# One weight transfer for two, dummy matmuls up to its landing, and one repeated matmul pair fewer

## The chip, the cores and the metric

The kernel runs on one core of a Trainium2 chip. The metric is the device time of one execution in microseconds (us). Timed runs of one kernel are compared with runs of the kernel before in the same rounds, on the same chip. "Span" is the length of one profiled execution; times within it count from its start.

## The reference, cut to what matters

```python
# x: [1, 384, 384, 384], dw: [1, 1, 384], pw: [384, 384], all bfloat16; k = 1, so no padding
out = x * dw[0, 0]                                  # depthwise, one tap
return jnp.einsum('bhwc,cd->bhwd', out, pw)         # pointwise: [147456, 384] x [384, 384]
```

The kernel folds dw into pw once, at its start, and then streams x through one matmul with the folded weight.

## The kernel before

Only the head (the first 7 us or so) is touched. SyncE issues pw in two transfers, then x:

```python
nc.scalar.dma_start(dw_row[:], ...).then_inc(s_dw, 16)
nc.sync.dma_start(pw_n[:, 0, :], pw[:P, :]).then_inc(s_pw[0], 16)
nc.sync.dma_start(pw_n[:, 1:3, :], pw[P:, :].rearrange("(k p) d -> p k d", p=P)).then_inc(s_pw[1], 16)
# ... x chunks follow on the same queue
```

TensorE runs dummy matmuls on zeros, and then folds dw into pw. sel_w is a selection matrix scaled by dw; a product of it with pw_n gives the folded weight in PSUM, two tiles of 64 rows at a time (a "pair"), six results in all, numbered i = 2k + r:

```python
idle_work(3)                      # loop, 3 trips of 4 dummy matmuls; needs only zeros
# ... three small matmuls for dw
idle_work(1)
times = {(1, 1): 3, (2, 0): 3}    # pairs that are repeated to keep TensorE busy
for k in range(3):
    if k < 2: nc.tensor.wait_ge(s_pw[k], 16)
    nc.tensor.wait_ge(s_sw, k + 1)                 # sel_w of this k
    for r in range(2):
        if k == 2: nc.tensor.wait_ge(*w_done[r])   # its PSUM bank has been copied out
        for v in [0, 1] * times.get((k, r), 1):
            mm = nc.tensor.matmul(PS[(k + 1) % 2][:, 2 * r + v, :D], lhsT=sel_w[...], rhs=pw_n[...], ...)
        mm.then_inc(s_w)
with nc.tensor.Fori(0, NS // 2, 1) as it:          # the body: 288 supertiles of 48 matmuls
    ...
```

Six PSUM-to-SBUF copies make w_r of the results: the second on VectorE, the others on ScalarE, one after another. The body's first matmul waits for the first four copies (they hold its first weights, and two of them free the PSUM banks that it writes) and for the first transpose of x on VectorE. `...` marks cuts.

## Time and profile before

| | us |
|---|---|
| time, three runs at first | 574.9, 575.14, 576.55 |
| time, these three and three more, taken with the changed kernel | median 576.16 |
| span of the profiled execution | 574.1 |
| body's first matmul | 7.21 |
| half-rate stretch of the body, up to full clock at 8.08 | 0.87 |
| start of the last matmul to the end | 5.1 |

TensorE starts its groups of four matmuls 0.30 to 0.32 us apart at first and 0.162 us apart from about 8.1 us on; below these are called half and full rate, or half and full clock.

The page's groups and chain and the head's timeline are shown in the prediction below. A group line reads: source line, engine, operation, tiles, shapes and count, then busy time in us, mean duration in ns, and idle time before the group with what ended most of it. A chain line reads: start, length, what was waited for. In a line of the stretches view each engine's busy time is followed by the number of its instructions that touch the stretch.

### The profile page before, as it was taken

How to read it: one execution, taken by the hardware profiler on the slowest of the kernel's cores; microseconds unless marked ns; L12 is line 12 of the kernel's file. 1: busy time of each engine (PE TensorE's matmuls, PEld its weight loads, DVE VectorE, ACT ScalarE, POOL GpSimd, SP SyncE). 2: the span in 40 equal slices, each digit the busy share in tenths (PEclk: the TensorE clock that was granted, in tenths of full speed). 3: DMA queues.
4: the chain of work that ended last, by engine and by line, in shares of the span. 5: the costliest groups of instructions: out<-in, count | busy, mean ns of one | idle time of the engine just before them, and what ended most of it. 6: DMA issues, size and time to landing. Idle time of an engine off the chain costs nothing.

```text
span 574.1 us, 29692 instructions
## 1 busy us (share of the span) xinstructions
PE 567.5 (99%) x13863; PEld 334.3 (58%) x13863; DVE 508.2 (89%) x583; ACT 419.1 (73%) x296; POOL 0.9 (0%) x8
## 2 busy tenths in 40 slices
PE   8999999999999999999999999999999999999996
PEld 4555555555555555555555555555555555555553
DVE  7889888988988898899889888988988898899884
ACT  6777777777777777777777777777777777777775
POOL 0000000000000000000000000000000000000000
PEclk9999999999999999999999999999999999999999
DMA  8999999999999999999999999999999999995996
GB/s 327 442 404 408 431 415 423 436 429 405 383 411 412 391 400 428 398 390 402 426 385 400 398 430 403 390 393 419 396 395 424 400 388 392 421 397 172 414 386 241
DMA packets 25929, 226.88 MB, mean 395 GB/s; under 512 B 1214, under 2 KB 5695, under 8 KB 22079
## 3 DMA queue, kind: packets, MB, share of 16 engines
q1 hardware_dynamic: 25916, 226.79, 98.1%
q14 instruction: 10, 0.07, 0.0%
q8 instruction: 1, 0.02, 0.0%
q10 hardware_dynamic: 2, 0.00, 0.0%
HBM read 113.54 MB, written 113.25 MB: 395 GB/s over the span
## 4 chain that ended last, share of the span: by engine, by line
PE 98%; DMA 1%; ACT 0%; DVE 0%; SPq 0%; issue 0%
PE ps L167 97%; DMA pw_n<-in_pw_dram 1%; PE ps L218 0%; DMA out_dram<-O 0%; ACT O L309 0%; DVE O L306 0%; SPq L132 0%; SPq L339 0%; SPq L100 0%
## 5 line engine op out<-in xcount | busy, mean ns | idle before, releaser
L167 PE MATMUL ps<-w_r,T 32*128 32x384 bf16 x13824 | 562.2, 321 | 0.0
L260 DVE STREAM_TRANSPOSE T<-X 128x384 uint32<-128x384 uint32 x576 | 505.0, 878 | 56.0 <-DMA X<-in_x_dram 1.4
L309 ACT CAST O<-ps 128x1536 bf16<-128x1536 f32 x288 | 413.6, 1436 | 148.1 <-PE ps L167 148.1
L167 PEld LDWEIGHTS ps<-w_r,T 32*128 32x128 bf16 x13824 | 332.5, 93 | 229.9 <-issue 1.0
L273 ACT CAST w_r<-ps 128x768 bf16<-128x768 f32 x5 | 3.9, 800 | 1.5 <-PE ps L218 1.5
L218 PE MATMUL ps<-pw_n,sel_w 64*128 64x384 bf16 x20 | 3.6, 518 | 0.5 <-DVE sel_w L288 0.3
L306 DVE CAST O<-ps 128x768 bf16<-128x768 f32 x1 | 1.0, 957 | 3.0 <-DMA out_dram<-O 3.0
L184 PE MATMUL ps<-zero 32*128 32x384 bf16 x16 | 1.8, 493 | 1.4 <-POOL zero L234 1.4
L218 PEld LDWEIGHTS ps<-pw_n,sel_w 64*128 64x128 bf16 x20 | 1.2, 131 | 2.6 <-DMA pw_n<-in_pw_dram 1.5
L246 ACT ACT_TABLE_LOAD x1 | 1.3, 1283 | 1.5 <-SPq L100 1.5
L278 DVE TENSOR_REDUCE sel<-eye 128x64 f32<-128x128 bf16 x1 | 0.3, 289 | 1.8 <-POOL eye L236 1.8
L184 PEld LDWEIGHTS ps<-zero 32*128 32x128 bf16 x16 | 0.5, 99 | 2.0 <-issue 2.0
L273 DVE CAST w_r<-ps 128x768 bf16<-128x768 f32 x1 | 1.0, 958 | 0.5 <-PE ps L218 0.5
L288 DVE TENSOR_SCALAR sel_w<-sel,dw_f 128x256 bf16<-128x256 f32 x3 | 0.9, 350 | 0.0
L285 DVE COPY dw_f<-ps 128x3 f32<-128x3 f32 x1 | 0.2, 160 | 0.8 <-PE ps L199 0.8
L236 POOL TENSOR_SCALAR_AFFINE_SELECT eye<-ones 128x128 bf16<-128x128 bf16 x1 | 0.3, 292 | 0.1
L246 ACT COPY warm<-warm 128x1 f32<-128x1 f32 x2 | 0.3, 189 | 0.0
L199 PEld LDWEIGHTS ps<-ones,dw_row 1*128 1x128 bf16 x3 | 0.2, 100 | 0.2 <-issue 0.2
L234 POOL MEMSET zero<- 128x192 uint32 x1 | 0.3, 258 | 0.0
L199 PE MATMUL ps<-ones,dw_row 1*128 1x1 bf16 x3 | 0.2, 160 | 0.0
L235 POOL MEMSET ones<- 128x128 bf16 x1 | 0.2, 204 | 0.0
L328 POOL MEMSET const-bfloat16-1.0<- 128x1 bf16 x1 | 0.1, 102 | 0.0
(4 smaller groups left out, 0.4 us busy)
## 6 DMA issues: line engine op xcount, KB each, us to landing
X<-in_x_dram SPq DMA_DIRECT2D x26, 3840.0 KB, 21.6
out_dram<-O SPq DMA_DIRECT2D x26, 3840.0 KB, 27.6
X<-in_x_dram SPq DMA_DIRECT2D x2, 1536.0 KB, 17.2
out_dram<-O SPq DMA_DIRECT2D x2, 1536.0 KB, 13.8
X<-in_x_dram SPq DMA_DIRECT2D x3, 768.0 KB, 7.6
out_dram<-O SPq DMA_DIRECT2D x3, 768.0 KB, 10.7
X<-in_x_dram SPq DMA_DIRECT2D x1, 2304.0 KB, 19.4
out_dram<-O SPq DMA_DIRECT2D x1, 2304.0 KB, 11.3
```

The lines of the kernel that those rows point to most:

```text
L167: mm = nc.tensor.matmul(PS[s][:, q, :D], lhsT=Ts[s][32 * q : 32 * q + 32, b, par::2], rhs=w_r[32 * q : 32 * q + 32, b, par, :], start=(b, ...
L184: nc.tensor.matmul(PS[0][:, i, :D], lhsT=zero[32 * i : 32 * i + 32, 0:P], rhs=zero[32 * i : 32 * i + 32, :], start=True, stop=True, tile_p ...
L199: mm = nc.tensor.matmul(PS[1][:, 0, D + k : D + k + 1], lhsT=dw_row[:, P * k : P * k + P], rhs=ones[0:1, 0:1], start=True, stop=True,)
L218: mm = nc.tensor.matmul(PS[(k + 1) % 2][:, 2 * r + v, :D], lhsT=sel_w[64 * v : 64 * v + 64, k, r, :, :].rearrange("p q w -> p (q w)"), rhs ...
L234: nc.gpsimd.memset(zero[:].bitcast(U32), 0).then_inc(s_zero)
L236: nc.gpsimd.affine_select(out=eye[:], in_=ones[:], pattern=[[-1, P]], compare_op=mybir.AluOpType.is_equal, fill=0.0, base=0, channel_multi ...
L246: c = nc.scalar.copy(warm[:, s + 1 : s + 2], warm[:, 0:1])
L260: ins = nc.vector.transpose(out=Tw[:, 3 * h : 3 * h + 3], in_=Xw[:, :, j, 96 * h : 96 * h + 96].rearrange("p k (b w) -> p b k w", w=32),)
L273: o = nc.vector.tensor_copy(out, in_) if e == 0 else nc.scalar.copy(out, in_)
L288: nc.vector.tensor_scalar_mul(sel_w[:, k], sel[:].unsqueeze(2).to_broadcast([P, 2, 4, 32]), dw_f[:, k : k + 1]).then_inc(s_sw)
L306: e = nc.vector.tensor_copy(Ov[:, nq:4, j, :], PS[s][:, nq:4, :D])
L309: a = nc.scalar.copy(Ov[:, 0:nq, j, :], PS[s][:, 0:nq, :D])
```

## The change

Its intent, as far as the edit tells: save one transfer issue, and keep TensorE busy without a gap up to the landing of pw, so that its clock comes to full rate earlier; the repeat is then less needed.

```diff
-        nc.sync.dma_start(pw_n[:, 0, :], pw[:P, :]).then_inc(s_pw[0], 16)
-        nc.sync.dma_start(pw_n[:, 1:3, :], pw[P:, :].rearrange("(k p) d -> p k d", p=P)).then_inc(s_pw[1], 16)
+        nc.sync.dma_start(pw_n[:], pw.rearrange("(k p) d -> p k d", p=P)).then_inc(s_pw, 16)
...
-        idle_work(1)
-        times = {(1, 1): 3, (2, 0): 3}
+        idle_work(3)
+        nc.tensor.wait_ge(s_pw, 16)
+        times = {(1, 1): 3, (2, 0): 2}
         for k in range(3):
-            if k < 2:
-                nc.tensor.wait_ge(s_pw[k], 16)
```

More of the change, by code (lines that the diff above doesn't have):

```diff
@@ L89 @@
     s_dw = nc.alloc_semaphore("s_dw")
-    s_pw = [nc.alloc_semaphore(f"s_pw{h}") for h in range(2)]
+    s_pw = nc.alloc_semaphore("s_pw")
     s_df = nc.alloc_semaphore("s_df")
```

## The prediction

> **What bounds the kernel now.** I read three things in this order: the groups of instructions with the chain that ended last (what sets the end), the timeline of the first 8 us (all that the diff touches), then the stretches of the main matmul line (how fast it runs, and from when).
>
> ```profile
> L167 PE MATMUL ps<-w_r,T 32*128 32x384 bf16 x13824 | 562.2, 321 | 0.0
> L260 DVE STREAM_TRANSPOSE T<-X 128x384 uint32<-128x384 uint32 x576 | 505.0, 878 | 56.0 <-DMA X<-in_x_dram 1.4
> ...
> L218 PE MATMUL ps<-pw_n,sel_w 64*128 64x384 bf16 x20 | 3.6, 518 | 0.5 <-DVE sel_w L288 0.3
> ```
>
> The main matmuls (L167) never wait: idle before them is 0.0. VectorE's transposes waited for an x transfer for 1.4 us in all, at the start. So although the DMA engines are busy 0.98 of the span, they keep up, and TensorE sets the pace from its first L167 matmul to its last. The stretch from 100 to 200 us holds 2464 weight loads, four to a group that runs at once on four row tiles: 616 groups in 100 us, 0.1623 us each. 13824 / 4 = 3456 groups x 0.1623 = 561.0 us. What remains of the 574.1 us span is a head of 7.2 us, a tail of 4.7 us (last matmul near 569.4, then copy, store and exit), and about 1 us of slow groups and drain. The change touches neither the 561 nor the tail. Its ceiling is the part of the head that it can shorten, plus matmuls that run at a slow clock.
>
> The chain of waits names the head:
>
> ```profile
> 1.47 3.03 DMA pw_n<-in_pw_dram
> 4.49 0.05 issue
> 4.54 2.74 PE ps L218 x12
> 7.28 558.25 PE ps L167 x11413
> ```
>
> It says second pw transfer, then weight preparation, then body. The timeline shows that this is not the only path into 7.2 us:
>
> ```profile
> 1.01 0.39 SPq L132 DMA_DIRECT2D pw_n<-in_pw_dram  x1
> 1.47 0.42 SPq L133 DMA_DIRECT2D pw_n<-in_pw_dram  x1
> 1.92 3.75 SPq L113 DMA_DIRECT2D X<-in_x_dram  x7
> 2.74 0.51 PE L184 MATMUL ps<-zero 32*128 32x384 bf16 x4
> 3.08 0.88 DVE L288 TENSOR_SCALAR sel_w<-sel,dw_f 128x256 bf16<-128x256 f32 x3
> 3.55 0.16 PEld L218 LDWEIGHTS ps<-pw_n,sel_w 64*128 64x128 bf16 x4 [0.70 <-DMA pw_n<-in_pw_dram]
> 4.54 0.13 PEld L218 LDWEIGHTS ps<-pw_n,sel_w 64*128 64x128 bf16 x4 [0.82 <-DMA pw_n<-in_pw_dram]
> 6.04 0.80 ACT L273 CAST w_r<-ps 128x768 bf16<-128x768 f32 x1 [0.16 <-PE ps L218]
> 6.24 10.29 DVE L260 STREAM_TRANSPOSE T<-X 128x384 uint32<-128x384 uint32 x12 [0.84 <-DMA X<-in_x_dram]
> 7.21 9.03 PE L167 MATMUL ps<-w_r,T 32*128 32x384 bf16 x208
> ```
>
> The first L167 matmul needs three ScalarE copies (the third runs 6.04 to 6.84) and the first transpose, which starts when x lands (6.24) and takes 0.86, so ends at 7.10. The later of the two is the transpose; 7.21 follows it by 0.1 us. The weight path has about 0.27 us to spare. TensorE meanwhile stands idle twice: 3.25 to 3.55, and 4.40 to 4.54, with only loosely packed work before.
>
> **The clock.** The stretches of L167 alone show the rest:
>
> ```profile
> 7.20:8.10 0.90, 0.89 (x12) 0.44 (x16) 1.00 1.01 416
> 8.10:9.00 0.90, 0.90 (x28) 0.55 (x24) 1.00 1.01 423
> ```
>
> The same 0.90 us holds 12 matmuls and then 28. The starts in the trace are 0.30 to 0.32 us apart per group up to 8.12 and 0.162 after it, and the trace's record of full clock begins at 8.08 (the clock column prints 1.00 before it too, so durations are the better witness). So 0.87 us of body ran at half rate in this execution, a loss of 0.87 / 2 = 0.43 us.
>
> **What the Trainium skill says.** "TensorE: Matmul & The Clock Gate", section "Part 1: The HAM clock gate": the array starts at half clock and is released after a busy window of about 3.4 us; the window is free-running, so the moment depends on its phase at kernel start. The trace agrees with the factor of two (0.32 against 0.162 us). It also fits the window: 8.08 less 3.41 is 4.67, just after TensorE became continuously busy at 4.54, while the window 1.25 to 4.66, in which TensorE shows 2.77 us busy of 3.41 with its modelled ends (less in streaming), did not release it. "DMA: Bandwidth & Descriptors", section "Queues, rings and completion order": descriptors of one queue are consumed in ring order, so x comes behind pw. The trace agrees: nearly all 768-byte pw packets finish before the 3072-byte x packets begin. Same page, "Why a DMA increments its semaphore by 16 and not by 1": a transfer is done when its slowest engine is. The trace shows it: of the second pw transfer's landings fifteen are in by 3.88 us and the last at 4.49; of the first x chunk fifteen by 5.53 and the last at 6.22.
>
> **The change part by part.**
> 1. One pw transfer for two. Bytes and packets stay (288 KB, 384 of 768 bytes). SyncE saves one issue: x is issued at about 1.47 instead of 1.92, 0.45 us earlier. But the engines were fed almost without a break from 2.02 us on (the second transfer's packets follow the first's by about 0.1 us, x's first packet comes 6 ns after an engine's pw finished), so I give x only 0.1 to 0.2 us of that: landing near 6.1.
> 2. The first weight matmuls now wait for the whole transfer. Before they were free at 3.43 by sel_w and ran at 3.58; now pw lands in one piece at T. 24 packets per engine x 36 ns = 0.86 us from 2.02, plus the roughly 0.6 us of starting stalls and completion, plus the late engine: T = 3.8 to 4.2 us. From T, the ScalarE path is: two matmul pairs and drain 0.55, copy 0.80, copy 0.80, copy 0.80, so the third copy ends at T + 2.95 to 3.0, i.e. 6.8 to 7.2, against 6.84 before. The weight path gives its slack away, and with a late T it becomes the bound.
> 3. Dummy loop of three in place of one: two more trips at 0.43 us (the spacing of the first loop's weight loads, 1.40, 1.84, 2.27). TensorE is then busy from 2.74 to about 4.1, which covers the wait. They cost nothing unless pw lands before about 4.05, then up to 0.2 us.
> 4. One repeat of the third block's first pair fewer: one pair, 0.32 us at half clock. It comes after what the third copy waits for, so it is off both paths; near zero.
>
> Start of the body: later of transposes (6.1 + 0.86 + 0.1 = 7.06) and weights (6.8 to 7.2, plus 0.1), so 7.1 to 7.2, a gain of 0.05 (range -0.2 to +0.3).
>
> Clock: with TensorE packed from 1.43 on, the first window that counts may begin anywhere within 3.41 us after 1.43 and releases the clock between 4.84 and 8.25, nearly always before the body begins. Before, the packed stretch began at 4.54, so release came between 7.95 and 11.36, by phase. Loss in the body is half of (release - 7.21): 0.37 to 2.07 us, mean 1.2; after, about 0.1. That is an estimate from the window the skill states. The profiled run, with 0.43, would be a lucky one; the spread of the three timed runs before (574.9 to 576.55, 1.65 us wide) is the width this predicts (1.7). The mean of the three is 575.5; less 1.1 for the clock and 0.05 for the start gives 574.4. If the denser head only sometimes passes, it is nearer 574.9. I take 574.5.
>
> **The rivals.**
> *Transfer hidden anyway:* x alone sets 7.21, the clock is released when it was, and nothing moves: 575.1 to 575.5. For it: x's landing is the last event before the body in the trace. Against it: the half-rate groups after 7.21 are real and the change fills the idle time before them.
> *A new wait:* pw in one piece lands late (its slowest engine), the first copy starts 0.5 us later than 4.12 and the third copy passes the transpose. For it: the late engine shows on both transfers. With T = 4.5 the body starts at 7.55: plus 0.35, partly paid back by the clock; 574.8 to 575.8.
> *DMA becomes the bound:* at 0.98 busy a faster TensorE could run into late x or O buffers. Against it: no transpose waits for x after the head, and half to one microsecond in 575 changes no rate. No effect.
> *The dummy work does not suffice:* the loop's branch leaves about 0.11 us in each 0.43, so the window may still fail; then the only effect is the start, 575.0 to 575.5.
>
> **Range and chances.** I give the clock story 0.6, hidden anyway or insufficient dummy work 0.3, a late pw 0.1. Centre 574.5, with phase alone able to move a run by a microsecond and medians of few runs: 573.8 to 575.5. A 2% change would be 11.5 us, more than the whole head; so within 2% at 0.98, and 0.01 on each side for a disturbed run.
>
> **What the profile after would show.** One pw issue, and x issued near 1.47; x landing (first transpose) at 6.0 to 6.2; pw landing near 4.0 with the dummy matmuls running up to it; weight pairs 0.16 us apart instead of 0.32 at least in their later part; the first L167 groups 0.162 apart from the start; L167 busy down from 562.2 to about 561.7; body starting at 7.0 to 7.3 and a tail of 4.7 unchanged. The prediction is wrong if the pairs in the head and the first groups are still 0.32 us apart (dummy work insufficient), if the first copy starts after 4.9 (pw late), or if L167 shows idle time later in the run (transfers now bind).

## The result, and the profile after

Six runs of the changed kernel: 575.22 to 575.92, median 575.36. Six of the kernel before: 574.9 to 576.55, median 576.16. The ratio is 0.9992, with a 95% interval of 0.9979 to 1.0005: the same, within noise. The means are 575.42 and 575.87, 0.45 us apart. The prediction had 574.5, a gain of 1 us over the mean of before's first three runs (575.5). The absolute time falls in its range; the gain that it explained does not appear.

The page of the changed kernel, the groups that answer to those of before:

```profile
L166 PE MATMUL ps<-w_r,T 32*128 32x384 bf16 x13824 | 561.8, 321 | 0.1
L258 DVE STREAM_TRANSPOSE T<-X 128x384 uint32<-128x384 uint32 x576 | 506.2, 882 | 54.0 <-DMA X<-in_x_dram 2.4
...
L216 PE MATMUL ps<-pw_n,sel_w 64*128 64x384 bf16 x18 | 3.0, 510 | 0.1
```

The body's busy time is 561.8 us, as foreseen (561.7), against 562.2. VectorE waits 2.4 us for x instead of 1.4, and the body does not feel it: its idle time is 0.1. The chain of the changed kernel:

```profile
1.01 3.03 DMA pw_n<-in_pw_dram
4.05 0.05 issue
4.09 2.96 PE ps L216 x18
7.05 0.12 issue
7.18 557.91 PE ps L166 x13728
```

The whole of pw lands at 4.04, 0.45 us before the second transfer of the kernel before did; but the weights then take 3.1 us to the body in place of 2.7. The body starts 0.04 us earlier than in the profile before. Its timeline shows why the weights take longer:

```profile
1.01 0.45 SPq L132 DMA_DIRECT2D pw_n<-in_pw_dram  x1
1.52 3.49 SPq L113 DMA_DIRECT2D X<-in_x_dram  x7
2.74 1.28 PE L183 MATMUL ps<-zero 32*128 32x384 bf16 x12
4.09 2.96 PE L216 MATMUL ps<-pw_n,sel_w 64*128 64x384 bf16 x18
4.63 3.80 ACT L271 CAST w_r<-ps 128x768 bf16<-128x768 f32 x5 [1.56 <-PE ps L216]
5.83 1.55 DVE L258 STREAM_TRANSPOSE T<-X 128x384 uint32<-128x384 uint32 x2
7.18 9.12 PE L166 MATMUL ps<-w_r,T 32*128 32x384 bf16 x220
```

ScalarE's first copy starts at 4.63 instead of 4.12, and from there the copies follow each other without a gap (3.80 us for five, none waiting again): three of them end at 7.03. Before, the first copy was under way when the second transfer landed (4.49). VectorE's transpose no longer waits for x (it landed at 5.00) and ends 0.5 us before the body starts. The stretches of the body's line in the changed kernel:

```profile
7.20:8.10 0.90, 0.90 (x24) 0.68 (x28) 1.00 1.06 423
8.10:9.00 0.90, 0.90 (x32) 0.62 (x24) 1.00 0.97 403
```

No thin first stretch: 24 matmuls against 12 before. The trace records full clock from 6.82 us, before the body starts. So in this one execution the body's clock and start went as predicted, and saved 0.43 us of half rate and 0.04 us of start. Two signs did not: the weight pairs stayed 0.32 us apart up to the last one, at 6.63 us, and x landed at 5.00 us where 6.0 to 6.2 was foreseen. The span fell from 574.15 to 573.70, by 0.45. The question is what one execution is worth.

### The profile page after: what moved, and what is told of

Read it like the earlier page. It is cut to its first block, busy times and chain, and to the rows that moved or that the text cites. A ratio compares the mean times of both kernels' runs of the same rounds, so it can differ in the third digit from the quotient of the medians.

```text
span 573.7 us, 29706 instructions
## 1 busy us (share of the span) xinstructions
PE 567.3 (99%) x13869; PEld 414.9 (72%) x13869; DVE 509.3 (89%) x583; ACT 418.8 (73%) x296; POOL 0.9 (0%) x8
## 4 chain that ended last, share of the span: by engine, by line
PE 98%; DMA 1%; ACT 0%; DVE 0%; issue 0%; SPq 0%
PE ps L166 97%; DMA pw_n<-in_pw_dram 1%; PE ps L216 1%; DMA out_dram<-O 0%; ACT O L307 0%; DVE O L304 0%; SPq L337 0%; SPq L100 0%
## 5 line engine op out<-in xcount | busy, mean ns | idle before, releaser
L166 PE MATMUL ps<-w_r,T 32*128 32x384 bf16 x13824 | 561.8, 321 | 0.1
L166 PEld LDWEIGHTS ps<-w_r,T 32*128 32x128 bf16 x13824 | 412.9, 93 | 149.2 <-issue 0.7
```

What stands on the lines that cost most here:

```text
L166: mm = nc.tensor.matmul(PS[s][:, q, :D], lhsT=Ts[s][32 * q : 32 * q + 32, b, par::2], rhs=w_r[32 * q : 32 * q + 32, b, par, :], start=(b, ...
```

## The experiments

In each trace I took four numbers: when pw was complete (the last of its sixteen landings), when the body started, when full clock was granted, and the length of the body from its first matmul's start to its last one's. **The body's length is 561.41 to 561.46 us plus half of its half-rate time in all 17 traces**, with half-rate times from 0 to 2.49 us. So "body start plus half of the half-rate time" is all that the head costs, and I call it the head cost. (Times read from the traces are in part cut, not rounded, at the second decimal, so a view can show 0.01 more.)

The windows of the clock show too: the records of full clock are 566.612, 563.199 and 580.266 us long, which is 166, 165 and 170 times 3.413 us. From a trace's release time (the moment when full clock is granted) I can therefore count back in windows of 3.413 us and work out how busy TensorE was in the window that brought full clock, and in the one before it that didn't. For this I take the first 0.32 us (the spacing of pairs at half clock) after each start of a matmul of 384 columns, counting overlaps once; after a matmul of fewer columns, in proportion less. Their share of the window I call the streaming share. The three one-column matmuls for dw count for nothing in it; had each counted for 0.32 us, as in the expectation of `e5_duty_384`, shares of windows that hold them would be 0.03 higher.

### Control: both kernels again

`c_before` is the kernel before and `c_after` the changed kernel, both without an edit.

> The kernel before, unchanged, as a control and for a second trace of its head. Both theories: ratio 1.000 within 0.002. Clock theory (the moment of full clock is random against the kernel's start, and before loses time to it): the runs spread over 1 to 2 us, and in this new trace full clock comes at another time than 8.08 us, somewhere in 4.7 to 11.4. Landing theory (the spread comes from late DMA engines in the head): the clock comes near 8.1 again, and the start of the body moves from 7.21 to anywhere in 6.4 to 7.3 with the landings of x and of the second pw transfer.

> The changed kernel, unchanged, for more runs and a second trace. Clock theory: full clock at another time than 6.82 us, within 4.8 to 8.3, so nearly no half-rate groups in the body; runs within 0.8 us of each other, 0.5 to 1 us below before on average (ratio 0.9983 to 0.9992). Landing theory: body starts 3.1 us after pw lands, ratio 0.999 to 1.001.

Measured: the unchanged copy of before has a ratio of 1.0013 to before (0.9993 to 1.0034), the changed kernel 1.0009 (0.9993 to 1.0025). A kernel compared with itself is off by 0.13%, 0.75 us; so the times cannot settle half a microsecond, and the traces must. Two expectations on the times failed here: the runs of the copy of before spread over 3.8 us in place of 1 to 2, and those of the changed kernel over 3.1 us in place of 0.8, with a ratio above the 0.9983 to 0.9992 foreseen. Full clock came at 9.35 us in the copy of before, in place of 8.08, and at 7.93 in the changed kernel, in place of 6.82: the moment is a matter of chance. The stretches of the body in the copy of before:

```profile
7.20:8.10 0.90, 0.90 (x16) 0.40 (x20) 1.00 1.02 423
8.10:9.00 0.90, 0.90 (x16) 0.41 (x12) 1.00 1.03 430
9.00:9.90 0.90, 0.90 (x24) 0.53 (x20) 1.00 1.11 464
```

Two thin stretches and part of a third: 2.24 us at half rate, 1.12 us lost. But the window from 2.52 to 5.94 us in that trace had a streaming share of 0.74 and did not bring full clock, and in the changed kernel the window from 1.11 to 4.52, with 0.73, did not either.

In this copy x landed at 5.42 us and its first transpose ended at 6.31, yet the body started at 7.11. So x is not what sets the start. In both traces of before the start is 2.72 us after the second landing of pw (4.49 and 4.39), and 0.46 us after the start of TensorE's last weight pair. The chain of the copy says the same:

```profile
4.44 2.74 PE ps L218 x16
7.18 558.92 PE ps L167 x12607
```

### The transfer alone, and the filling alone

`e1_one_transfer` is the changed kernel with the dummy loop and the repeat of before:

```diff
-        idle_work(3)
+        idle_work(1)
         nc.tensor.wait_ge(s_pw, 16)
-        times = {(1, 1): 3, (2, 0): 2}
+        times = {(1, 1): 3, (2, 0): 3}
```

> The merged transfer alone: dummy loop of one, third repeat kept. TensorE then stands idle from 3.25 to about 4.0 us. If the dummy matmuls carry the gain (clock theory): 0.3 to 1 us slower than the changed kernel, no better than before (ratio to before 1.000 to 1.001), full clock as late as in before, at 7.9 to 11 us in most executions. If the transfer carries it: same as the changed kernel within 0.2 us, ratio 0.999 to 0.9995.

`e2_fill_two_transfers` is the kernel before with its gaps filled:

```diff
-        idle_work(1)
-        times = {(1, 1): 3, (2, 0): 3}
+        idle_work(2)
+        times = {(0, 1): 2, (1, 1): 3, (2, 0): 3}
```

> Two transfers as before, but the idle time of TensorE filled: dummy loop of two in place of one, and the first block's second pair done twice. If the filling carries the gain: 0.3 to 1 us faster than before (ratio 0.998 to 0.9995), perhaps faster than the changed kernel, as the first weight copy need not wait for all of pw (third copy 2.35 us after the second landing in place of 3.0). If the transfer carries it: ratio 1.000 within 0.0005.

Measured: both 1.0019 (1.0006 to 1.0032). Their means, 576.46 and 576.54, are those of the unchanged copy of before in the same call (576.58), so neither is shown to be slower or faster than it; the changed kernel's mean there was 576.12. Both expectations of a difference went unanswered by the times. The traces answered: in `e1_one_transfer` full clock came at 6.76 us, though TensorE was idle from 3.25 to 3.99: that window's streaming share was 0.81. This contradicts the prediction's step that a window must be filled from end to end. In `e2_fill_two_transfers` it came at 7.81; the window before, with 0.73, had failed. Body starts: 3.13 us after pw in the first, 2.73 after the second landing in the second.

### How busy is busy enough?

To measure the limit by itself, without a matter of phase, the changed kernel got a long dummy loop before the weights: 45 trips of 384 columns, 60 of 256, 90 of 128.

```diff
-        def idle_work(n):
+        def idle_work(n, cols=D):
...                                  # PS[0][:, i, :cols] and rhs=zero[..., :cols]
-        idle_work(3)                # the second loop
+        idle_work(45, 384)          # or (60, 256), or (90, 128)
```

> How busy must TensorE be to get the full clock, measured by itself: the changed kernel with 45 trips of the dummy loop of 384 columns before the weights (body 15 us later or less; the result stays right). In the six traces so far windows of 3.413 us with a streaming share of 0.77 or less did not bring the full clock and windows with 0.81 or more did. Threshold theory (about 0.8 is enough): trips are 0.385 us apart with 0.32 streaming, share 0.83, so full clock comes at the first window end whose window holds enough, between 4.7 and 8.3 us, while the loop still runs. Rival (the dummy matmuls are too loose or, being zeros, don't count; only real, gapless matmuls release it): 0.385 us apart for all 45 trips, full clock only 3.4 to 6.8 us after the weight matmuls begin near 20 us.

> The same with 60 trips of 256 columns: 0.213 us of streaming in a trip of 0.28 to 0.30 us (estimate: the loop's 0.065 us over 0.32, or a little more), share 0.71 to 0.77. Threshold theory: not released in the loop; full clock comes after the weight matmuls and the body are under way, up to 6.8 us after the loop ends, and the body's span is 561.43 us plus half its half-rate time. If it is released in the loop, the threshold is lower than the six traces say.

> The same with 90 trips of 128 columns: 0.107 us in a trip of about 0.17, share near 0.62. Threshold theory: never released in the loop, as for 256 columns; body loses 0.3 to 2 us to half rate. Rival (any steady activity releases it): full clock between 4.8 and 8.3 us.

Measured: a trip takes 0.388 us on average whatever its columns, so my estimates of a shorter trip were wrong, and the streaming shares of a trip are 0.83, 0.55 (0.213 / 0.388) and 0.28. Over whole windows, where the four matmuls of a trip start up to 12 ns apart, they come to 0.86, 0.56 to 0.59 and 0.28 to 0.31. With 384 columns full clock came at 7.92 us, in the loop; the window before, with 0.73, had failed. With 256 it did not come in the 22.9 us of the loop, and with 128 not in 34.5 us; it came at 28.27 and 43.20, after the real matmuls had begun at 26.0 and 37.6. The group lines of the weight matmuls, which follow the loop, show it by their mean durations. With 384, 256 and 128 columns:

```profile
L216 PE MATMUL ps<-pw_n,sel_w 64*128 64x384 bf16 x18 | 1.8, 323 | 0.2 <-ACT w_r L271 0.2
```

```profile
L216 PE MATMUL ps<-pw_n,sel_w 64*128 64x384 bf16 x18 | 2.7, 476 | 0.0
```

```profile
L216 PE MATMUL ps<-pw_n,sel_w 64*128 64x384 bf16 x18 | 3.1, 518 | 0.1
```

323 ns is full clock, 518 half, and 476 a release on the way. So zeros count, a gapless window is not needed, and steady activity is not enough: the limit lies between the highest share that failed and the lowest that passed. The rivals of both kinds (only real matmuls count; any activity counts) fall. The number of matmuls in a window is not what counts either: it is the same in all three loops. Nor is the busy time of the profile, whose ends are modelled: from 8 to 11 us the loop of 256 columns shows 2.97 of 3.00 us busy, and the clock was not released.

### Two more looks at the kernel before, and the repeat put back

> A further trace of the kernel before. Threshold theory (a window of 3.413 us needs a streaming share of about 0.8): with the starts of the matmuls as traced, full clock comes between 6.6 and 10.0 us, wherever the window happens to lie. The prediction's reading (a window filled from end to end, so packed from 4.54 on): between 7.95 and 11.36 us. A release below 7.9 or a passed window below 0.95 speaks for the first. Body start 2.72 us after the second pw landing; body 561.43 us plus half of its half-rate time.

> The same as the run before it, for one more phase of the window: release between 6.6 and 10.0 us by the threshold theory, 7.95 to 11.36 by the prediction's reading.

Measured: full clock at 7.10 and at 5.24 us. Both are below the 7.95 that the prediction's reading gives; the second is also below the 6.6 that I had expected from the limit of 0.8, because I had worked that out with the landing of the first trace, and here pw was complete at 4.05 instead of 4.49. Its passed window had a share of 0.78. With 0.74 failed (`c_before`) and 0.78 passed the limit is bracketed, for this measure of busy: in all 17 traces the passed windows have 0.78 or more and the failed ones 0.74 or less. The chain of `c_before3`:

```profile
4.12 2.25 ACT w_r L273 x3
6.37 0.14 issue
6.51 555.96 PE ps L167 x13680
```

With pairs at full clock TensorE's own path is no longer the last, and ScalarE's three copies are: the body starts at 6.51, the earliest of all.

`e10_repeat_kept` is the changed kernel with `(2, 0): 3` in place of `(2, 0): 2`.

> The changed kernel with the third repeat put back: what is the removed repeat worth? Prediction: nothing, it is off both paths. TensorE's own path (pairs 0.32 us apart at half clock, then 0.46 to drain before the body's first matmul, as in before): the body starts 3.36 us after pw lands, in place of 3.13, if full clock comes later than the last pair (after about 7.1 us); 3.13 to 3.2 if it comes before 6.8 us, as the pairs are then 0.16 apart.

Measured: pw complete at 4.04, full clock at 7.33, body start at 7.39, which is 3.36 us after pw, as expected. Its weight pairs and its body:

```profile
4.08 3.38 PE L216 MATMUL ps<-pw_n,sel_w 64*128 64x384 bf16 x20
7.39 1.80 PE L166 MATMUL ps<-w_r,T 32*128 32x384 bf16 x40
```

The removed repeat is worth 0.23 us when the clock comes late (3.36 against the 3.13 of `after` and `c_after`; one trace). The prediction gave it nothing.

### Two attempts at a faster head

`e8_two_plus_one` sends two thirds of pw first and the last third after it; `e9_x_between` puts the first x chunk between them.

```diff
-        nc.sync.dma_start(pw_n[:, 0, :], pw[:P, :]).then_inc(s_pw[0], 16)
-        nc.sync.dma_start(pw_n[:, 1:3, :], pw[P:, :].rearrange(...)).then_inc(s_pw[1], 16)
+        nc.sync.dma_start(pw_n[:, 0:2, :], pw[: 2 * P, :].rearrange(...)).then_inc(s_pw[0], 16)
+        nc.sync.dma_start(pw_n[:, 2, :], pw[2 * P :, :]).then_inc(s_pw[1], 16)   # e9: after x chunk 0
...
-        idle_work(1)
-        times = {(1, 1): 3, (2, 0): 3}
+        idle_work(2)
+        times = {(1, 1): 3, (2, 0): 2}
-            if k < 2: nc.tensor.wait_ge(s_pw[k], 16)
+            if k != 1: nc.tensor.wait_ge(s_pw[k // 2], 16)
```

> A version meant to beat both: two transfers, but two thirds of pw first (first and second block) and the last third after it, dummy loop of two, third repeat twice. In the traces the body starts 3.13 us after the whole pw lands in the changed kernel (third ScalarE copy, plus 0.14) and 2.72 us after the second landing in before (TensorE's own pairs plus 0.46 to drain). If these waits are what sets the start, two thirds landing near 3.5 us give a body start at 6.5 to 6.7 us, 0.45 us before the changed kernel's 7.09 to 7.17, unless x (5.4 to 6.2 in before) lands late. If x sets the start as the prediction said, the start stays at x landing plus 0.95. The time moves by 0.1%, less than the noise that the unchanged copy showed (ratio 1.0013, 0.9993 to 1.0034).

> Second attempt at a version that beats both: two thirds of pw, then the first x chunk, then the last third of pw, so that neither x (6.61 us in the run with two thirds first) nor the weights are late. If the landings set the start: x lands at 4.6 to 5.2 us, two thirds of pw near 3.55, body start at 6.65 to 6.8 us, 0.3 to 0.5 us before the changed kernel's 7.09 to 7.17, span 573.2 to 573.4 us in an execution without half-rate groups and with the usual 5.07 us tail. If DVE or another wait sets it, the start stays at 7.1. Times: ratio 0.998 to 1.000, likely within the noise.

Measured: ratios 0.9992 (0.9969 to 1.0014) and 0.9996 (0.9981 to 1.0011), no difference shown. The chain of the first, then of the second:

```profile
2.01 4.60 DMA X<-in_x_dram
6.62 0.02 issue
6.64 0.87 DVE T L260
7.51 0.09 issue
7.60 557.90 PE ps L167 x13728
```

```profile
2.01 4.34 DMA pw_n<-in_pw_dram
6.35 0.05 issue
6.40 1.14 PE ps L219 x6
7.54 558.99 PE ps L168 x13727
```

The two thirds landed at 3.57 and 3.60, as hoped, but in the first x was complete only at 6.61, and the transpose set the start at 7.60. In the second x was complete at 6.09 and the last third of pw at 6.35, though fifteen of their sixteen landings were in by 4.52 and 5.75. Each saved wait was given to a transfer behind it. Both missed the start that was hoped for (6.5 to 6.7 and 6.65 to 6.8): the body started at 7.60 and at 7.47, and in the second full clock came only at 9.85. In neither trace was the head better than the changed kernel's; no version here is shown to beat both.

### The changed kernel three times more

> A third trace of the changed kernel. Theory now held: pw lands at 3.9 to 4.15 us, body starts 3.13 us later (7.05 to 7.3), full clock between 4.6 and 8.1 us, so half-rate time at most 0.9 us; start plus half of it 7.05 to 7.6, no lower than the better half of before's four traces (6.51, 7.00). If the change does help as predicted, the sum is below 7.1 in most of the three.

> As the run before it, for a further phase: start 7.05 to 7.3, release 4.6 to 8.1 us, sum 7.05 to 7.6.

> As the two before it: start 7.05 to 7.3, release 4.6 to 8.1 us, sum 7.05 to 7.6.

Measured: as the theory now held expects, but for one trace (`c_after2`) with pw and the start a little earlier (3.86 and 7.04). Its sum is below 7.1 in one of the three, where "most" would have spoken for the prediction. All traces of the two kernels, in us:

| trace | pw complete | first x chunk | body start | full clock | half of half-rate time | head cost |
|---|---|---|---|---|---|---|
| before | 4.49 | 6.22 | 7.21 | 8.08 | 0.43 | 7.64 |
| c_before | 4.39 | 5.42 | 7.11 | 9.35 | 1.12 | 8.23 |
| c_before2 | 4.19 | 5.62 | 6.91 | 7.10 | 0.10 | 7.00 |
| c_before3 | 4.05 | 5.46 | 6.51 | 5.24 | 0 | 6.51 |
| mean | 4.28 | 5.68 | 6.93 | | 0.41 | 7.35 |
| after | 4.04 | 5.00 | 7.17 | 6.82 | 0 | 7.17 |
| c_after | 3.96 | 4.89 | 7.09 | 7.93 | 0.42 | 7.51 |
| c_after2 | 3.86 | 4.82 | 7.04 | 6.33 | 0 | 7.04 |
| c_after3 | 3.93 | 5.08 | 7.06 | 7.66 | 0.30 | 7.36 |
| c_after4 | 4.03 | 5.70 | 7.16 | 6.97 | 0 | 7.16 |
| mean | 3.96 | 5.10 | 7.10 | | 0.14 | 7.25 |

The clock's loss falls by 0.27 us on average, and the body starts 0.17 us later on average: 0.10 us remain, 0.02% of the time. With four traces of before that differ by 1.7 us, not even the sign of this 0.10 is shown. What the change does in these traces is narrow the head cost, from 6.51 to 8.23 down to 7.04 to 7.51; the timed runs do not show it, as the next part explains.

### What else spreads the times

The trace with the best head, `c_before3`, took 576.6 us. Its tail did that. SyncE's wait for the last store in `c_before3`, then in the changed kernel's first trace:

```profile
SPq L142 <- DMA out_dram<-O: 3.8, 1, 3.8
```

```profile
SPq L141 <- DMA out_dram<-O: 2.0, 1, 2.0
```

From the last matmul's start to the end, 13 of the 17 traces take 5.06 to 5.08 us; `c_before`, `c_before2`, `c_before3` and `e7_duty_128` take 5.99, 6.23, 6.91 and 7.20, and the difference is all in the last store: its issue comes 1.42 to 1.43 us after that start in every trace, its landing after 3.73 to 3.75 in the thirteen and 4.66, 4.90, 5.58 and 5.87 in the four. What makes it late I did not find; other traces with two pw transfers (before, `e2_fill_two_transfers`, `e8_two_plus_one`) have the short tail, so I do not put it down to the change. It is larger than the effect under study.

## Why the prediction was right or wrong

**The bound: right.** The body never waits, and its length at full clock is 561.4 us against the 561.0 worked out. The head and the clock in the body's first microseconds are all that the change can move, and the 98% for "within 2%" followed from that.

**The clock, wrong in size; this is the step that failed.** The prediction put it: "Before, the packed stretch began at 4.54, so release came between 7.95 and 11.36, by phase. Loss in the body is half of (release - 7.21): 0.37 to 2.07 us, mean 1.2; after, about 0.1." The mechanism is there: a free-running window of 3.413 us, a release by chance of its phase, half of the half-rate time lost. But I read "busy" as gapless. A streaming share of 0.78 was enough, and 0.74 was not; the loose head of before reaches that in many phases. Four traces of before released at 5.24 to 9.35 us and lost 0 to 1.12 us, mean 0.41, in place of 1.2. After the change the mean of five is 0.14 against the 0.1 foreseen. So the term of 1.1 us measured 0.27. Few traces were taken, but the size does not hang on their luck: reckoned over all phases of the window, with the matmul starts of each trace and a limit of 0.745 to 0.775, before loses 0.29 to 0.43 us on average and the changed kernel 0.06 to 0.07 (an estimate from these nine traces).

**The start, wrong in its bound.** "The later of the two is the transpose; 7.21 follows it by 0.1 us. The weight path has about 0.27 us to spare." There was a third path: TensorE's own pairs and the 0.46 us from the last pair to the body's first matmul. It gave 7.21 as well (6.75 + 0.46), and in `c_before`, where x was early, it gave 7.11 (6.66 + 0.45). The chain of waits had said so, and I put it aside for a coincidence in one trace. The start follows pw, which in the profiled execution was the latest of four (4.49 against 4.05 to 4.39); so the foreseen gain of 0.05 us is a loss of 0.17 on average over these traces, most of it from `c_before3`, where the clock came early.

**The merged transfer: right.** pw complete at 3.86 to 4.04 (foreseen 3.8 to 4.2), the third copy 2.99 to 3.03 us later (2.95 to 3.0), body start 7.04 to 7.17 (7.1 to 7.2). "The weight path gives its slack away" is what happened, though it was not slack. x gained 0.58 us on average where I gave it 0.1 to 0.2; nothing waited for it. (That pw packets "nearly all" finish before x packets begin is put loosely: in the trace of before the first x packet began at 3.10 us, when 133 of the 384 pw packets had still to end; by 3.50 us 380 of pw had begun, and 12 of x.)

**The dummy loop: right, but for the pairs.** Its last trip is over at 3.83 us in the changed kernel's first trace, before pw lands. In `c_after2`, where pw landed at 3.86, the first pair started 0.09 us after the landing in place of 0.05, so there the loop cost about 0.05 us. The full rate that it was to bring to the later weight pairs came after the last pair in four of the five traces, and just before it in `c_after2`. The rival that it is too loose falls with `e5_duty_384`, at 0.83.

**The removed repeat: wrong.** "Off both paths; near zero" holds when the clock comes early; `e10_repeat_kept` shows 0.23 us when it comes late, by the same third path.

**The base.** The three times known before (mean 575.5) were read as base plus clock loss, and their width of 1.65 us as the width of the phase. In the traces the last store alone varies by as much as 2 us, and that the two widths agreed was chance. Whether the 0.45 us between the first six runs of each kernel are real stays open: the interval includes no change, and a kernel against its own copy differed by more.

## What to carry to other kernels

When a start-up stage has several paths that end within a few tenths of a microsecond, write out every one of them, TensorE's own issue and drain included, and take more than one trace before believing which is last. A transfer made whole was complete earlier here, but work that could begin on its first part began later: compare the end of the chain behind it, not the landing. Where the gain depends on a free-running phase, ask how much of a window must be filled; filling it beyond that gained 0.27 us here, not 1.1.

## What the Trainium skill lacked or had wrong

- "TensorE: Matmul & The Clock Gate", "Part 1: The HAM clock gate": it speaks of a busy window of about 3.4 us of sustained activity and doesn't say how busy. The runs show a streaming share of 0.74 failing and 0.78 passing, dummy matmuls on zeros counting, and 22.9 us at 0.55 without a release. Its free-running window of 3413 ns agrees: records of full clock are 165, 166 or 170 windows long.
- The same page, same section, says that the cold count should not be fitted, as it varies from run to run. The runs agree, and more widely than the ±500 ns that the section gives for the transition: release at 5.24 to 9.35 us for one unchanged kernel.
- "TensorEngine Tiling (Array Packing)", "Key Properties", says that a change of tiling mode drains TensorE, but no page has the time from the last 64-row pair to the first matmul on 32-row tiles: 0.45 to 0.46 us at half clock where TensorE's own path was last (before, `c_before`, `c_before2`, `e10_repeat_kept`), against 0.32 from pair to pair. That it is this drain is argued, not shown.
- No page has the cost of a hardware loop's trip on TensorE (it would belong to "Advanced Engine Details and Errata", "Control Flow Timing", which times branches alone): 0.388 us on average for four matmuls, the same for 128, 256 and 384 columns, and the same at full clock.
- "DMA: Bandwidth & Descriptors", "Rules for kernel authors", advises to coalesce many small transfers, above all under 64 KB; it has no word on work that could begin on the first of them. Here, with transfers of 96 and 192 KB, the merged one was complete 0.32 us earlier on average (3.96 against 4.28) and the body began no earlier; the second x chunk came later in the changed kernel (7.73 to 8.04 against 6.65 to 7.18 us), although it was issued 0.4 us earlier. Of the experiments with the merged transfer two show it too (7.50 and 7.93) and three do not (6.0 to 6.5), so its cause is open.
